# List-scheduled attention and MoE kernel: the planner is told of shared banks of the score tiles, and two due times are moved

## Chip, core, metric

One NeuronCore of one Trainium2 chip runs the whole program. The metric is device time in microseconds (us), median of the runs; less is better.

## What is computed

Two batches, 8 heads, 768 positions, 64 features per head. Queries and keys are each assigned to one of 16 clusters of their head, attention is allowed only inside a cluster, and the result goes through two MLP blocks without a residual:

```python
mask = q_assign[:, :, :, None] == k_assign[:, :, None, :]
scores = np.where(mask, scale * np.matmul(q, k.transpose(0, 1, 3, 2)), -1e9)
attn = softmax(scores); x = attn @ v            # (2, 8, 768, 64) -> (1536, 512)
h = x @ w_in                                     # 512 -> 2048
x = piecewise_quadratic(h) @ w_out               # 2048 -> 512
out = ((x @ w1) * (x @ w2) @ w3) @ w_out2        # 512 -> 1024 -> 1024 -> 512
```

The weights arrive as 64-bit floats and are turned into 32-bit ones on the chip. w3 and w_out2 are multiplied together once (into `wp`).

## The kernel before

**Work.** For each batch there are four units (pairs of heads) and, in each unit, 12 score tiles of 128 queries by 768 keys: 48 score tiles a batch. A score tile s goes through a chain. TensorE writes the scores into PSUM, four matmuls (`s`, L819). VectorE takes the row maximum (`smax`, L827), GpSimd turns it into a bias (`sbias`, L832), ScalarE takes the exponent out of PSUM into the SBUF tile P (`sexp`, L840). In the first batch TensorE then transposes P back into the same PSUM tile, six matmuls (`spT`, L857), and ScalarE or VectorE copies that to `pt` (`sT`, L372 or L374), which frees the PSUM tile. Twelve such tiles end in two products with v (`pv`, L923) with their normalisers (`ro`, L906).

Beside it the first batch's stage holds 16 matmul groups of eight for w3 times w_out2 (`wp`, L1152), the conversion of those weights (L1061 to L1094), and, for the second batch's mask, two groups `am` (L526) with a VectorE chain behind each (`ah`, L540 to L570; its step 4 is two matmuls, L562). `am`, `ah` step 4 and the transposes of v (`vpT`, L750) use PSUM tiles of the same ring as the scores. Matmuls on the identity with nothing to do with the result (L474) keep TensorE occupied where it has no other work early on.

After the first batch's attention, its MLP blocks run on TensorE together with the second batch's attention, then the second batch's MLP blocks (L1208).

**PSUM.** The first batch's ring `("sc", 0)` has four tiles of 768 fp32 columns. `banks` (L292) cuts them in pairs out of tiles of three banks of 512 columns: the first of a pair has bank 1 and half of bank 2, the second the other half of bank 2 and bank 3. So the two tiles of a pair share a bank. The second batch's ring has two tiles with banks of their own. The semaphores, which the framework adds when the program is built, keep apart two engines on one bank of such a tile, whichever halves they use.

**Order.** Every step is entered with `add(...)`: a name, the engines that may do it with a cost in us, a due time, its needs, and what it takes from and frees in rings of buffers. `Plan.order` plays the program through with these costs. Whenever an engine is free it starts the ready step with the earliest due time; a step that isn't ready (`can`) is passed over. What comes out is a fixed order of instructions for each engine's queue, and a queue runs strictly in that order on the chip. The plan knows needs and rings. It does not know of shared banks.

**Due times.** Score tile s of the first batch is due at `slot(s)`, in equal steps from T_A0 = 14 to T_H[0] - 10 = 150 (2.83 each); its later steps are due 1 to 3.5 later. Scores of the second batch are due from T_H[0] - 6 = 154 to T_X1 = 390. `wp` products are due from 45 on, every 7.5. The second batch's mask steps are due from T_A1 = 115 on (keys) and 118 (queries), their eight loads on the SP queue (`al`, L518) 4 earlier; each load waits until the splits of the first batch's unit that sits in the same buffer are done. MLP steps of the first block are due in 56 equal steps from T_H[0] = 160 to T_H[1] = 435, those of the second from 435 to 660.

Of the kernel before, what the change touches and what calls it, by code (L numbers as in the profile page):

```python
# [36 lines left out]
class Plan:  # L37
# [17 lines left out]
    def __init__(self, rings):  # L55
        self.rings, self.ops, self.names, self.last = dict(rings, lane=self.LANES), [], {}, {}

    def add(self, name, engines, due, fn, needs=(), takes=(), frees=(), behind=None, moves=()):

        assert name not in self.names, name
        engines = {e: c if isinstance(c, tuple) else (c, 0.0) for e, c in engines.items()}
        self.names[name] = len(self.ops)
        lanes = [("lane", (name, i)) for i in range(len(moves))]
        prev = self.last.get(behind) if behind else None
        if behind:
            self.last[behind] = len(self.ops)
        lags = {}
        for x in needs:  # L70
            lag, x = x if isinstance(x[0], float) else (0.0, x)
            lags[x] = max(lag, lags.get(x, 0.0))
        self.ops.append([name, engines, due, fn, lags, list(takes) + lanes, list(frees) + lanes, prev, moves])

    def order(self):
        ops, n = self.ops, len(self.ops)
# [9 lines left out]
        engines = ("DMA", "PE", "ACT", "DVE", "POOL")  # L86
# [9 lines left out]
        ring_free = data_free = port_free = self.FIRST  # L96
        done, out, started, now = [], [], [False] * n, self.FIRST

        def can(i):
            if ready_at[i] > now or (ops[i][7] is not None and not started[ops[i][7]]):  # L100
                return False
            need = {}
            for r, _ in ops[i][5]:
                need[r] = need.get(r, 0) + 1
            for r, m in need.items():
                t, size = taken[r], self.rings[r]
                if len(t) + m > size:
                    for x in t[max(0, len(t) - size):max(0, len(t) - size + m)]:
                        if freed.get((r, x), 1e9) > now:
                            return False  # L110
            return True

        def soon(e, i):

# [9 lines left out]
        while len(out) < n:  # L124
            again = True
            while again:
                again = False
                for e in queue:
                    if free_at[e] > now:
                        continue  # L130
                    skipped, pick = [], None
                    while queue[e]:
                        it = heapq.heappop(queue[e])
                        if started[it[1]]:
                            continue
                        if can(it[1]) and not (ops[it[1]][8] and issue_free[e] > now):
                            pick = it
                            break
                        skipped.append(it)
                    for it in skipped:  # L140
                        heapq.heappush(queue[e], it)
                    if pick is None:
                        continue
                    if now < self.START and soon(e, pick[1]):
                        heapq.heappush(queue[e], pick)
                        continue
                    i, again = pick[1], True
                    started[i] = True
                    free_at[e] = now + ops[i][1][e][0]
                    if e == "POOL" or (e == "DVE" and ops[i][0][0] in self.PORT):  # L150
                        free_at[e] += max(0.0, port_free - now)
                        port_free = free_at[e]
                    end = free_at[e] + self.LAT.get(e, 0.0)
                    for ring, data in ops[i][8]:
                        ring_free = max(now, ring_free) + ring
                        data_free = max(ring_free + 0.65, data_free) + data
                        end = max(end, data_free + 0.95)
                    if ops[i][8]:
                        issue_free[e] = ring_free
                    for r, x in ops[i][5]:  # L160
                        taken[r].append(x)
                    heapq.heappush(done, (end, i, 0))
                    out.append((now, len(out), i, e))
            if not done:
                assert all(started), "the rings are too small"
                break
            now = min([done[0][0]] + [t for t in (*free_at.values(), *issue_free.values()) if t > now])
            while done and done[0][0] <= now:
                t, i, who = heapq.heappop(done)
                if not who:  # L170
                    for x in ops[i][6]:
                        holds[x] -= 1
                        if not holds[x]:
                            freed[x] = t
                for k, lag in [(who, 0.0)] if who else users[i]:
                    if lag:
                        heapq.heappush(done, (t + lag, i, k))
                        continue
                    waits[k] -= 1
                    if not waits[k]:  # L180
                        ready_at[k] = t
                        for e, (_, late) in ops[k][1].items():
                            heapq.heappush(queue[e], (ops[k][2] + late, k))
# [5 lines left out]
def cluster_attention_moe_kernel(  # L189
# [121 lines left out]
    plan = Plan(RINGS)  # L311
# [5 lines left out]
        "xs": ROW, "xr": ROW, "os": ROW,  # L317
    }

    def add(name, engines, due, fn, needs=(), takes=(), frees=(), behind=None, moves=None):  # L320
        kind = name if isinstance(name, str) else name[0]
        if moves is None:
            moves = MOVES.get(kind, ()) if "DMA" in engines else ()
        plan.add(name, engines, due, fn, needs, takes, frees, behind, moves)

    T = {}

# [63 lines left out]
    N_IDLE, N_IDLE1 = 90, 30  # L391
    W_SIDE = 1
    LAG_W, LAG_RO, LAG_RI, LAG_K2 = 0.5, 0.5, 1.5, 0.5
    T_AA, T_A1 = 14.0, 115.0
    T_A0, T_W, DT_W = 14.0, 45.0, 7.5
    T_H = [160.0, 435.0, 660.0]
    T_X1 = 390.0


# [192 lines left out]
    for b in range(B):  # L592
        u0 = b * NP
        s0 = T_A1 if b else slot(0) - T_AA
        for wi, w in enumerate("kq"):
            t = s0 + 3.0 * wi
            for j in range(NP):
# [2 lines left out]
                    ("al", b, w, j), {"DMA": 0.5}, t + 0.3 * j - 4.0, raw_load(b, w, j, "a"),  # L600
                    [(x, j, h) for x in left for h in range(2)] + [("qh0", j)] if b else [],
                )
            add(("am", b, w), {"PE": 2.7}, t + 0.9, a_mm(b, w, range(NP)), ["c_put"] + [("al", b, w, x) for x in range(NP)], [(("sc", 0), ("a", b, w))])
            steps = [("DVE", 0.95), ("DVE", 0.87), ("DVE", 0.87), ("DVE", 0.87), ("PE", 0.66 if b == 0 else 0.45), ("DVE", 0.87)]
            if w == "q":
                steps.append(("ACT", 0.83))
            for st, (e, c) in enumerate(steps):
                needs = [("ah", b, w, st - 1)] if st else [("am", b, w)]
                if st == 1 and w == "q":
                    needs.append(("ah", b, "k", 2))  # L610
                add(
                    ("ah", b, w, st), {e: c}, t + 1.5 + 0.1 * st, a_hot(b, w, st), needs,
                    {0: [(("P", 0), ("a", b, w))], 2: [(("phl", 0), ("a", b, w))], 4: [(("sc", 0), ("a2", b, w))],
                     5: [(("P", 0), ("m", w))] if b else []}.get(st, []),
                    {0: [(("sc", 0), ("a", b, w))], 2: [(("P", 0), ("a", b, w))],
                     5: [(("phl", 0), ("a", b, w)), (("sc", 0), ("a2", b, w))]}.get(st, []),
                )
            if b:
                add(("ap", w), {"DMA": 0.5}, t + 2.5, a_put(w), [("ah", b, w, 5 + "kq".index(w))], frees=[(("P", 0), ("m", w))])
# [142 lines left out]
    for u, (b, j) in enumerate(units):  # L762
# [28 lines left out]
        p = slot(u * NG * NS + NS - 1)  # L791
        add(("vl", u), {"DMA": 0.5}, p - 14.0, v_load(u), ([("s", u * NG * NS - V_AHEAD)] if u else [("al", 0, "q", NP - 1)]), [("raw", ("v", u))])
        if whole(u):
            add(("vpT", u), {"PE": 0.65}, p - 3.0, v_pT(u), [("vl", u), "c_put"], [(("sc", b), ("v", u))], [("raw", ("v", u))])
            add(
                ("vT", u), {"ACT": 0.73, "DVE": (0.87, LATE)}, p - 2.0, v_put(u), [("vpT", u)], [("vn", u)],
                [(("sc", b), ("v", u))],
            )
            continue
        add(("vm", u), {"DVE": 1.4}, p - 8.0, v_max(u), [("vl", u)])  # L800
# [48 lines left out]
    def by_pe(s):  # L849
        return s % PE_EVERY[s // NU] == 0  # L850
# [128 lines left out]
    for u, (b, j) in enumerate(units):  # L979
        for g in range(NG):  # L980
            for r in range(NS):
# [5 lines left out]
                    [("k2", u, h), ("klo", u, h)] + ([("k2h", u, h), ("q1h", u, h)] + ([("qh0", u)] if h else []) if by_copy(u) else []),  # L987
                    [(("sc", b), s)],
                    [((x, b), (u, h)) for x in ("k1", "q1", "kq2")] if t == NQ - 1 and g == NG - 1 else [],
                )  # L990
                add(("smax", s), {"DVE": 0.87}, p + 1.0, s_max(s, b), [("s", s)])
                add(("sbias", s), {"POOL": 0.3}, p + 1.0, s_bias(s), [("smax", s)])
                add(
                    ("sexp", s), {"ACT": 0.89}, p + 2.0, s_exp(s, u, g, h, t), [("sbias", s)],
                    [(("P", b), s)] if by_pe(s) else [],
                )
                key, first = ("pt", (u, g, h)), [("pt", (u, g, h))] if t == 0 else []
                hi, lo = {"ACT": 0.73, "DVE": (0.87, LATE)}, {"DVE": 0.88}
                if by_pe(s):
                    add(("spT", s), {"PE": 0.65}, p + 3.0, s_pT(s, b), [("sexp", s), "c_put"], frees=[(("P", b), s)])  # L1000
                    if whole(u):
                        add(("sT", s), hi, p + 3.5, s_hi(s, u, g, h, t), [("spT", s)], first, [(("sc", b), s)], behind=key)
                        continue
                    add(("shi", s), hi, p + 3.5, s_hi(s, u, g, h, t), [("spT", s)], first, behind=key)
                    add(("sT", s), lo, p + 4.2, s_lo(s, u, g, h, t), [("shi", s)], frees=[(("sc", b), s)])
# [413 lines left out]
```

## Time and profile before

| | |
|---|---|
| median of 3 runs | 792.83 us (791.03 to 793.93) |
| profiled execution | 791.59 us |
| its span, first to last instruction | 789.6 us, so 1.99 us lie around it |
| TensorE busy in the span | 758.0 us (96%) |
| VectorE, ScalarE, GpSimd busy | 568.6 (72%), 448.8 (57%), 216.5 us (27%) |
| mean granted TensorE clock | 0.996 of full speed |

In the profile PE is TensorE's matmuls, DVE VectorE, ACT ScalarE, POOL GpSimd, SPq the SP queue. L819 is line 819 of the kernel. Idle time is given with the instruction whose end released it. A queue's idle time matters where its engine sets the end, here TensorE nearly throughout.

### The profile page before, as it was taken

Reading aid. Unit: us, or ns where it says so; the run is one execution under the profiler, and the core shown is the slowest. Engines: PE = TensorE matmul, PEld = TensorE weight load, DVE = VectorE, ACT = ScalarE, POOL = GpSimd, SP = SyncE. Lnnn points to the kernel's source line nnn. Section 1 sums busy time; section 2 is a strip of 40 time slices with the busy share of each in tenths; the row PEclk is TensorE's granted clock in tenths of the full one; section 3 lists DMA queues with packets and bytes.
Section 4 is the critical chain, followed back from the end, with each engine's and each line's share of the span. In section 5 each row is a group of like instructions: output and inputs, shape, how many; then the busy total and the mean of one; then the engine's idle time right before and its main releaser. Section 6 shows DMA issues by size and latency. Waiting matters only on the chain.

```text
span 789.6 us, 12412 instructions
## 1 busy us (share of the span) xinstructions
PE 758.0 (96%) x4593; PEld 665.0 (84%) x4593; DVE 568.6 (72%) x935; ACT 448.8 (57%) x804; POOL 216.5 (27%) x251
## 2 busy tenths in 40 slices
PE   7989899989999999999999999999999999999998
PEld 5864555545669898999989898999999999999998
DVE  7889686778789788999899999842655564644520
ACT  7478687754677566687677766631544353323311
POOL 0223233421243334555445544210211021000000
PEclk9999999999999999999999999999999999999999
DMA  8416564646378458777776888663222212221211
GB/s 335 143 47 217 176 202 139 226 129 203 121 211 165 94 127 156 206 199 160 209 215 178 224 200 203 167 182 108 72 68 55 73 60 68 68 66 54 67 61 61
DMA packets 100973, 112.78 MB, mean 143 GB/s; under 512 B 61489, under 2 KB 69681, under 8 KB 100913
## 3 DMA queue, kind: packets, MB, share of 16 engines
q1 hardware_dynamic: 78768, 52.48, 26.4%
q10 hardware_dynamic: 22144, 59.52, 24.9%
q8 instruction: 36, 0.59, 0.3%
q14 instruction: 25, 0.20, 0.1%
HBM read 73.70 MB, written 20.19 MB: 119 GB/s over the span
## 4 chain that ended last, share of the span: by engine, by line
PE 77%; DVE 9%; ACT 5%; issue 3%; DMA 3%; POOL 2%; SPq 0%; ACTq 0%; POOLq 0%; DVEq 0%
PE mo L1208 36%; PE sc L1208 15%; PE sc L819 7%; PE sc L857 4%; PE av L1208 4%; PE mo L1152 3%; PE av L931 3%; PE av L923 3%; DVE nm L827 2%; ACT P L840 2%; ACT pt L372 1%; PE mo L906 1%; DMA pt<-phl 1%; DVE wf L1077 1%; DMA kq<-in_qT_dram 1%
## 5 line engine op out<-in xcount | busy, mean ns | idle before, releaser
L1208 PE MATMUL mo<-X,whl 128*128 128x384 f32 x1188 | 216.3, 337 | 0.4 <-DVE G L377 0.4
L1208 PEld LDWEIGHTS mo<-X,whl 128*128 128x128 f32 x1188 | 205.2, 188 | 2.6 <-DVE G L377 1.0
L377 POOL TENSOR_TENSOR whl<-wf,whl 128x512 fp32r<-128x512 f32 x60 | 79.0, 1318 | 176.4 <-DVE whl L374 44.8
L1208 PE MATMUL mo<-G,whl 128*128 128x384 f32 x660 | 120.2, 337 | 0.0
L1208 PEld LDWEIGHTS mo<-G,whl 128*128 128x128 f32 x660 | 114.0, 188 | 1.6 <-issue 0.6
L827 DVE TENSOR_REDUCE nm<-sc 128x1 f32<-128x768 f32 x96 | 90.9, 951 | 29.8 <-PE sc L819 12.6
L1208 PE MATMUL sc<-X,whl 128*128 128x384 f32 x432 | 76.5, 335 | 0.0
L372 ACT ACTIVATE whl<-wf 128x512 fp32r<-128x512 f32 x69 | 43.5, 632 | 55.7 <-PE mo L1208 30.3
L1208 PEld LDWEIGHTS sc<-X,whl 128*128 128x128 f32 x432 | 75.1, 188 | 0.0
L840 ACT ACTIVATE P<-sc,nm 128x768 f32<-128x768 f32 x64 | 57.5, 900 | 21.1 <-POOL nm L832 11.5
L857 PEld LDWEIGHTS sc<-ident,P 128*128 128x128 f32 x384 | 43.5, 141 | 26.6 <-ACT P L840 10.6
L857 PE MATMUL sc<-ident,P 128*128 128x128 f32 x384 | 52.9, 277 | 12.8 <-ACT P L840 5.8
L832 POOL TENSOR_SCALAR nm<-nm 128x1 f32<-128x1 f32 x96 | 29.1, 303 | 131.4 <-DVE nm L827 123.5
L372 ACT ACTIVATE pt<-sc 128x768 f32<-128x768 f32 (+1 forms) x55 | 44.1, 811 | 35.0 <-PE sc L857 19.1
L819 PE MATMUL sc<-k,q 128*128 128x512 f32 (+1 forms) x192 | 55.6, 371 | 6.3 <-ACT pt L372 2.6
L1152 PE MATMUL mo<-wo,wf 128*128 128x512 f32 x128 | 58.3, 599 | 0.7 <-ACT rb L372 0.7
L1094 POOL TENSOR_TENSOR wf<-wf,w 128x512 int32<-128x512 int32 x32 | 44.2, 1382 | 53.7 <-DVE wf L1077 33.9
L377 DVE TENSOR_TENSOR whl<-wf,whl 128x512 fp32r<-128x512 f32 x52 | 36.9, 709 | 23.6 <-ACT whl L372 22.1
L819 PE MATMUL sc<-kq 80*128 80x512 f32 (+1 forms) x192 | 49.7, 340 | 0.0
L374 DVE CAST whl<-wf 128x512 fp32r<-128x512 f32 x43 | 18.8, 438 | 42.0 <-PE mo L1208 23.1
L1077 DVE SCALAR_TENSOR_TENSOR wf<-w,wf 128x512 uint32<-128x512 uint32 x64 | 48.1, 753 | 0.3
L819 PEld LDWEIGHTS sc<-k,q 128*128 128x128 f32 x192 | 31.6, 190 | 16.7 <-ACT pt L372 4.4
(155 smaller groups left out, 1220.0 us busy)
## 6 DMA issues: line engine op xcount, KB each, us to landing
wf<-wd ACTq DMA_DIRECT2D x64, 256.0 KB, 2.6
w<-in_w_out_dram ACTq DMA_DIRECT2D x24, 512.0 KB, 3.9
wd<-wf SPq DMA_DIRECT2D x48, 256.0 KB, 3.4
w<-in_w3T_dram ACTq DMA_DIRECT2D x16, 512.0 KB, 4.0
w<-in_w_in_dram ACTq DMA_DIRECT2D x16, 512.0 KB, 4.2
w<-in_w_dram ACTq DMA_DIRECT2D x16, 512.0 KB, 4.2
wf<-wp ACTq DMA_DIRECT2D x16, 256.0 KB, 2.9
kq<-in_kT_dram SPq DMA_DIRECT2D x8, 384.0 KB, 4.6
```

What stands on the lines that cost most here:

```text
L372: nc.scalar.activation(out=out, in_=in_, func=AF.Copy)
L377: (nc.gpsimd if e == "POOL" else nc.vector).tensor_tensor(out=out, in0=a, in1=b, op=ALU.subtract)
L819: nc.tensor.matmul(ps[:, n], q[0:n_rows, q0:q0 + 128], k[0:n_rows, n], start=first, stop=not first)
L827: nc.vector.tensor_reduce(out=nm, in_=T[("sc", b), s], axis=AX.X, op=ALU.max, negate=True)
L832: nc.gpsimd.tensor_scalar(out=tl[s, "nm"], in0=tl[s, "nm"], scalar1=SCALE, scalar2=EC, op0=ALU.mult, op1=ALU.add)
L840: nc.scalar.activation(out=new(("P", b), s).rearrange("p n s -> p (n s)") if by_pe(s) else T[("sc", b), s], in_=T[("sc", b), s], func=AF.E ...
L857: nc.tensor.transpose(T[("sc", b), s][:, c], p[:, c], ident)
L923: nc.tensor.matmul(acc[rows(h), :], vn[:, kt, rows(h)], T["pt", (u, g, h)][:, :, kt, :], start=(kt == 0), stop=(kt == KT - 1),)
L1077: nc.vector.scalar_tensor_tensor(out=w, in0=T[w64, i][:, :, 1], scalar=0xC0000000, in1=w, op0=ALU.bitwise_and, op1=ALU.bitwise_or)
L1094: nc.gpsimd.tensor_tensor(out=w, in0=w, in1=T[w64, i].bitcast(I32)[:, :, 0], op=ALU.add)
L1152: nc.tensor.matmul(acc, w[:, k4 * 128:(k4 + 1) * 128], wo2[:, hf * 4 + k4], start=(hf == 0 and k4 == 0), stop=(hf == 1 and k4 == 3),)
L1208: nc.tensor.matmul(acc, w[:, a, k4 * 128:(k4 + 1) * 128], rhs(c, k4), start=(first and k4 == 0 and n == 0), stop=(last and k4 == 3 and n = ...
```

## The change

No step is added or taken away. A step may name a tile in its new argument `near`. While the plan is made, a TensorE step with `near` isn't started as long as a step of another engine with `near` on the same pair of tiles is running, and the other way round. Two readers are not kept apart. It holds for the first batch's ring only. Steps with `near`: `am`, `ah` steps 0, 4 and 5, `vpT`, `vT`, `s`, `smax`, `sexp`, `spT`, `sT`. Besides, T_A1 goes from 115 to 105 and T_H[0] from 160 to 155 (and with it the first batch's scores to 14 to 145, 2.73 each, the second's to 149 to 390).

```diff
-    def add(self, name, engines, due, fn, needs=(), takes=(), frees=(), behind=None, moves=()):
+    def add(self, name, engines, due, fn, needs=(), takes=(), frees=(), behind=None, moves=(), near=None):
...
-        def can(i):
+        def can(i, e):
...
                         if freed.get((r, x), 1e9) > now:
                             return False
+            if ops[i][9]:
+                r, x = ops[i][9]
+                if until.get((r, pair(r, x), e != "PE"), 0.0) > now:
+                    return False
             return True
+
+        until = {}
+
+        def pair(r, x):
+            return (taken[r].index(x) if x in taken[r] else len(taken[r])) % self.rings[r] // 2
...
                     for r, x in ops[i][5]:
                         taken[r].append(x)
+                    if ops[i][9]:
+                        r, x = ops[i][9]
+                        until[r, pair(r, x), e == "PE"] = end
...
-        plan.add(name, engines, due, fn, needs, takes, frees, behind, moves)
+        plan.add(name, engines, due, fn, needs, takes, frees, behind, moves, (near if near and near[0] == ("sc", 0) else None))
...
-    T_AA, T_A1 = 14.0, 115.0
+    T_AA, T_A1 = 14.0, 105.0
     T_A0, T_W, DT_W = 14.0, 45.0, 7.5
-    T_H = [160.0, 435.0, 660.0]
+    T_H = [155.0, 435.0, 660.0]
...
+                    near=(("sc", 0), ("a" if st == 0 else "a2", b, w)) if st in (0, 4, 5) else None,
...
+                    near=(("sc", b), s),
                 )
-                add(("smax", s), {"DVE": 0.87}, p + 1.0, s_max(s, b), [("s", s)])
+                add(("smax", s), {"DVE": 0.87}, p + 1.0, s_max(s, b), [("s", s)], near=(("sc", b), s))
```

`am`, `vpT`, `vT`, `sexp`, `spT` and the first batch's `sT` get the same `near=` argument.

## Rows read from the trace of the kernel before

**Rows 1.** Busy time by stretch: us, busy of PE, PEld, DVE, ACT, POOL; clock, DMA share, GB/s
```profile
31.00:232.00 201.00, 181.64 (x996) 112.30 (x995) 158.28 (x246) 138.58 (x236) 66.00 (x84) 0.99 0.52 166
232.00:500.00 268.00, 264.70 (x1732) 246.82 (x1731) 246.60 (x394) 188.40 (x347) 119.08 (x132) 1.00 0.75 180
```

**Rows 2.** Waits of PE, 31 to 232 us: total us, times, longest us
```profile
PE sc L857 <- ACT P L840: 5.2, 8, 1.1
PE sc L819 <- ACT pt L372: 2.6, 4, 0.9
PE sc L857 <- DVE P L540: 2.6, 1, 2.6
PE sc L857 <- DVE nm L827: 2.3, 2, 1.5
PE sc L857 <- ACT pt L372: 2.1, 3, 1.7
PE sc L819 <- DVE nm L827: 1.5, 3, 0.5
PE sc L819 <- ACT P L840: 0.9, 1, 0.9
PE sc L819 <- DVE pt L374: 0.7, 2, 0.4
```

**Rows 3.** Timeline: start us, us, engine, line, operation [idle before <- releaser]
```profile
111.72 0.89 ACT L840 ACTIVATE P<-sc,nm 128x768 f32<-128x768 f32 x1
112.75 0.61 PE L819 MATMUL sc<-k,q 128*128 128x512 f32 x2 [0.92 <-ACT P L840]
```

**Rows 4.** Timeline of PE: the first and the last of three waits for an own result
```profile
45.33 0.88 PE L857 MATMUL sc<-ident,P 128*128 128x128 f32 x6 [0.72 <-ACT P L840]
...
67.03 1.76 PE L857 MATMUL sc<-ident,P 128*128 128x128 f32 x12 [1.14 <-ACT P L840]
```

**Rows 5.** Timeline of the longest wait, 164 to 176 us
```profile
164.42 0.59 ACT L372 ACTIVATE wf<-mo 128x512 f32<-128x512 f32 x1
...
167.57 0.98 DVE L540 STREAM_TRANSPOSE P<-sc 128x768 f32<-128x768 f32 x1 [0.17 <-ACT P L840]
...
168.61 1.27 PE L857 MATMUL sc<-ident,P 128*128 128x128 f32 x6 [2.61 <-DVE P L540]
...
170.97 4.29 PE L1152 MATMUL mo<-wo,wf 128*128 128x512 f32 x8
```

**Rows 6.** Busy time by stretch, as in rows 1, right behind that wait
```profile
170.00:172.00 2.00, 2.00 (x6) 1.29 (x6) 0.80 (x1) 0.73 (x1) 0.00 (x0) 0.50 0.76 250
```

**Rows 7.** Timeline of PE: the same three steps as in rows 5 at another place
```profile
127.42 0.88 PE L857 MATMUL sc<-ident,P 128*128 128x128 f32 x6
...
128.83 3.60 PE L1152 MATMUL mo<-wo,wf 128*128 128x512 f32 x8
```

**Rows 8.** Timeline of PE: the first and last of ten waits with a product ready
```profile
55.50 0.87 PE L857 MATMUL sc<-ident,P 128*128 128x128 f32 x6 [0.75 <-ACT P L840]
...
219.22 1.53 PE L857 MATMUL sc<-ident,P 128*128 128x128 f32 x12 [0.90 <-ACT P L840]
```

**Rows 9.** Waits of ACT and of DVE, 31 to 232 us: total us, times, longest us
```profile
ACT pt L372 <- DVE nm L827: 14.0, 6, 5.8
...
DVE nm L827 <- ACT P L840: 7.8, 7, 2.5
```

**Rows 10.** Timeline of the SP queue: the last load for the second batch's mask
```profile
154.07 0.33 SPq L518 DMA_DIRECT2D kq<-in_qT_dram  x1
```

**Rows 11.** Timeline, 213 to 223 us: the end of the first batch's attention
```profile
213.37 0.52 PE L819 MATMUL sc<-k,q 128*128 128x256 f32 x2
...
214.08 3.60 PE L1152 MATMUL mo<-wo,wf 128*128 128x512 f32 x8
...
220.59 3.60 PE L1152 MATMUL mo<-wo,wf 128*128 128x512 f32 x8
...
221.50 0.81 ACT L372 ACTIVATE pt<-sc 128x768 f32<-128x768 f32 x1
```

More of the change, by code (lines that the diff above doesn't have):

```diff
@@ L72, in add @@
             lags[x] = max(lag, lags.get(x, 0.0))
-        self.ops.append([name, engines, due, fn, lags, list(takes) + lanes, list(frees) + lanes, prev, moves])
+        self.ops.append([name, engines, due, fn, lags, list(takes) + lanes, list(frees) + lanes, prev, moves, near])
     def order(self):
@@ L135, in order @@
                             continue
-                        if can(it[1]) and not (ops[it[1]][8] and issue_free[e] > now):
+                        if can(it[1], e) and not (ops[it[1]][8] and issue_free[e] > now):
                             pick = it
@@ L318, in cluster_attention_moe_kernel, with add @@
     }
-    def add(name, engines, due, fn, needs=(), takes=(), frees=(), behind=None, moves=None):
+    def add(name, engines, due, fn, needs=(), takes=(), frees=(), behind=None, moves=None, near=None):
         kind = name if isinstance(name, str) else name[0]
@@ L602, in cluster_attention_moe_kernel @@
                 )
-            add(("am", b, w), {"PE": 2.7}, t + 0.9, a_mm(b, w, range(NP)), ["c_put"] + [("al", b, w, x) for x in range(NP)], [(("sc", 0), ("a", b, w))])
+            add(("am", b, w), {"PE": 2.7}, t + 0.9, a_mm(b, w, range(NP)), ["c_put"] + [("al", b, w, x) for x in range(NP)], [(("sc", 0), ("a", b, w))], near=(("sc", 0), ("a", b, w)))
             steps = [("DVE", 0.95), ("DVE", 0.87), ("DVE", 0.87), ("DVE", 0.87), ("PE", 0.66 if b == 0 else 0.45), ("DVE", 0.87)]
@@ L793, in cluster_attention_moe_kernel @@
         if whole(u):
-            add(("vpT", u), {"PE": 0.65}, p - 3.0, v_pT(u), [("vl", u), "c_put"], [(("sc", b), ("v", u))], [("raw", ("v", u))])
+            add(("vpT", u), {"PE": 0.65}, p - 3.0, v_pT(u), [("vl", u), "c_put"], [(("sc", b), ("v", u))], [("raw", ("v", u))], near=(("sc", b), ("v", u)))
             add(
                 ("vT", u), {"ACT": 0.73, "DVE": (0.87, LATE)}, p - 2.0, v_put(u), [("vpT", u)], [("vn", u)],
-                [(("sc", b), ("v", u))],
+                [(("sc", b), ("v", u))], near=(("sc", b), ("v", u)),
             )
@@ L994, in cluster_attention_moe_kernel @@
                     ("sexp", s), {"ACT": 0.89}, p + 2.0, s_exp(s, u, g, h, t), [("sbias", s)],
-                    [(("P", b), s)] if by_pe(s) else [],
+                    [(("P", b), s)] if by_pe(s) else [], near=(("sc", b), s),
                 )
@@ L999, in cluster_attention_moe_kernel @@
                 if by_pe(s):
-                    add(("spT", s), {"PE": 0.65}, p + 3.0, s_pT(s, b), [("sexp", s), "c_put"], frees=[(("P", b), s)])
+                    add(("spT", s), {"PE": 0.65}, p + 3.0, s_pT(s, b), [("sexp", s), "c_put"], frees=[(("P", b), s)], near=(("sc", b), s))
                     if whole(u):
-                        add(("sT", s), hi, p + 3.5, s_hi(s, u, g, h, t), [("spT", s)], first, [(("sc", b), s)], behind=key)
+                        add(("sT", s), hi, p + 3.5, s_hi(s, u, g, h, t), [("spT", s)], first, [(("sc", b), s)], behind=key, near=(("sc", b), s))
                         continue
```

## The prediction

> **What bounds the kernel now.** I began with the busy times by stretch. From 31 to 232 us, the first batch's attention with its `wp` products, TensorE is busy for 181.64 of 201 us; from 232 to 500 us for 264.70 of 268 [rows 1]. So TensorE sets the pace, and what it loses it loses in the first of these stretches: 201 - 181.64 = 19.4 us. The change acts in just that stretch, since only the first batch's ring is named in `near`. VectorE (158.28) and ScalarE (138.58) have more room there, on average.
>
> The second view is the list of TensorE's waits in the stretch [rows 2]. Nearly all of the 19.4 us stand before L819 (scores) and L857 (transposes): 5.2 + 2.6 + 2.6 + 2.3 + 2.1 + 1.5 + 0.9 + 0.7 = 17.9 us. The reader is to see what ended them. A score tile's own chain gives L857 one thing to wait for, its exponent (ACT P L840), and gives L819 one, the copy that frees its tile (L372 or L374). A transpose that waits for a row maximum (DVE nm), for another tile's copy (ACT pt) or for the mask's VectorE transpose (DVE P L540), and scores that wait for a maximum or an exponent, wait for somebody else's read. Those rows are 2.6 + 2.3 + 2.1 + 1.5 + 0.9 = 9.4 us. The timeline shows one: an exponent runs from 111.72 to 112.61, and scores that have no need of it start at 112.75 after 0.92 us of waiting [rows 3]. The other reader sits in the tile that shares the bank. The rest, 5.2 + 2.6 + 0.7 = 8.5 us, can be either. Counting the instructions of each line off against the written order, I find three waits for an own result among them, the first of 0.72 us and the last of 1.14 us [rows 4], 2.4 us in all. So **about 17.9 - 2.4 = 15.5 us are waits on a shared bank**, which the plan did not foresee: it put a step at the head of TensorE's queue that could not start, and what was ready behind it stood still.
>
> **The change, part by part.** No instruction is added or removed, DMAs included; the cost of the planning is paid when the program is built. What changes is order, and here and there which of two engines does a copy.
>
> *The knowledge of pairs.* Where a reader is under way in the pair, the planner passes over the score or transpose and takes another TensorE step. It saves the wait if such a step is ready. I take the `wp` products as the cover, since they write no shared bank. In ten of the waits the next product had its weights ready and its accumulator free by the written order: the first is the 0.75 us before the transpose at 55.50, the last the 0.90 us at 219.22 [rows 8], and the 0.92 us of [rows 3] is one. The largest is the 2.61 us before the transpose at 168.61, ended by L540; the copy that frees the accumulator for the product run at 170.97 was over at 164.42 + 0.59 = 165.01 [rows 5], before the wait began. Together the ten are 7.7 us. For the other 15.5 - 7.7 = 7.8 us I see no product to put there, so I leave them.
>
> *The clock.* Behind that 2.61 us the granted clock was 0.50, the lower of its two levels (1.2 against 2.4 GHz), from 170 to 172 us [rows 6]. Transpose, scores and product took 170.97 + 4.29 - 168.61 = 6.65 us there; the same three took 128.83 + 3.60 - 127.42 = 5.01 us elsewhere [rows 7]. If the wait goes, 1.6 us go with it.
>
> *What it costs.* A product of 3.60 us put first makes a ready score or transpose late, and all that hangs on it: the copy, the freed tile, the next scores. The trace has no price for a tile that is late on purpose. At the least it is nothing, as TensorE works meanwhile; at the most it is the whole 7.7 us, as another wait later. The nearest rows are the waits for own results, which are what lateness costs now: 2.4 us over 48 tiles, 0.05 each [rows 4]. For the ten displaced tiles I take three times that, 0.15 us each: 1.5 us.
>
> *The new waits in the plan.* A reader is now held back too, in the plan, while TensorE writes the pair. The chip does that anyway, so it adds no wait; it moves conversions of weights ahead on VectorE and ScalarE. I count nothing: both have over 40 us free in the stretch [rows 1]. Without that room it would be up to one read, about 0.9 us [rows 3], each time.
>
> *T_A1, 10 earlier.* Eight loads on SP, two `am` groups on TensorE and the mask's chain on VectorE get an earlier due time. The last of the loads went out at 154.07 [rows 10], and each has to wait for the splits of the unit whose buffer it fills; those splits move by 4 at most (slots of 2.73 for 2.83). So most of the 10 cannot be used. Behind a load that waits on the SP queue stand the stores of converted weights, which free the buffers of the next conversion; a load takes 0.33 us there, and eight are 2.6 us of a queue that is nearly empty. Nothing, between -1 and +1 us.
>
> *T_H, 5 earlier.* The second batch's scores and the first MLP block are due 5 earlier together, and their order against each other stays nearly what it was: they start more than 70 us after their due times anyway (154, against the 228 at which this stage is over). Covered by the full TensorE from 232 us on. Nothing, within 1 us either way by a new order.
>
> **The sum.** 7.7 + 1.6 - 1.5 = 7.8 us less. As TensorE works through 264.70 of the next 268 us [rows 1], I carry all of it to the end. The profiled execution took 791.59 us: 783.8. The median shown lies 1.24 us above it, so 785.0 us, 1% less. The most that the mechanism can bring is all 15.5 us and the clock's 1.6, 17.1 in all: 775.7. The least is nothing.
>
> **A rule that speaks against it.** VectorE waits for ScalarE's exponents, 7.8 us in seven waits, and ScalarE's copies for row maxima, 14.0 us in six [rows 9]. These are reads that wait for reads, and the change leaves them out of the plan. The Trainium skill, PSUM — Partial Sum Buffer, on bank collisions, counts two engines' reads of one bank as a collision too, so that reads have to be kept apart as well as a write from a read. The trace agrees with that rule: the two rows are such waits. By it, a plan that keeps only writes from reads is still wrong on the chip; what that would cost is the first rival.
>
> **The rivals.** *Reads against reads (no change).* The plan is true for TensorE but not for its feeders. Their waits, 14.0 and 7.8 us [rows 9], stay, so exponents and copies come later than planned, and the waits on banks turn into waits for own results. Then only the one long wait goes surely, 2.61 + 1.6 = 4.2 us, and half of that is paid back in late tiles: 792.83 - 2.1 = 790.7 us. For it: these waits are as large as TensorE's own. Against: they fall on engines that have 43 and 62 us free, and five of the eight rows of TensorE's waits cannot be waits for an own result at all.
>
> *Given back later (no change).* From 232 to 500 us VectorE is busy for 246.60 of 268 us, 92% [rows 1]. If TensorE comes there 8 us earlier with fewer weights converted ahead, VectorE sets the pace and takes the 7.8 us back: 792.8. Against: its work up to the stage's end shifts with TensorE's, since both go by the same tiles.
>
> *An empty end of the stage (slower).* The products are a stock of 16, and what is used early is missing later. The last scores start at 213.37, the last copy ends at 221.50 + 0.81 = 222.31: a chain of 8.9 us, filled by the two products at 214.08 and 220.59, 7.2 us [rows 11]. If both were moved ahead of the last scores, TensorE would stand for 7.2 us where nothing else is allowed to start, and the lower clock would follow: 7.2 + 1.6. With half of the ten waits saved (3.9), that is 792.83 + 8.8 - 3.9 = 797.7 us. It decides from the point at which no product is left when the 46th tile is written. Against: products are due up to 157.5, later than the last score (145), so the list tends to keep the last ones.
>
> **The numbers.** 0.64 for the forecast, with a range of its own from 778 to 789; 0.16 for reads against reads, 0.09 for given back later, 0.11 for the empty end. A measurement of this kernel tells about 0.5% from no change, 4.0 us. The forecast is faster, the next two are no change (0.25), the last is slower. For 8 in 10 I go from 778, some 2 us above the best that the waits allow, to 796, which takes in both cases of no change and the upper bound of the unknown costs; the rest of the empty end, and a gain near the maximum, are left out.
>
> **What would show it.** Right: TensorE's idle time from 31 us to the end of the first batch's attention falls from 19 to about 11 us; the rows of L857 and L819 released by DVE nm, ACT pt and DVE P shrink most; products stand directly behind the places of the old waits; no stretch after 31 us has a clock of 0.5; the attention of the first batch ends some 8 us earlier, and all that follows is shifted by as much. Reads against reads: the idle time stays near 19 us, with ACT P before L857 as the largest row. Given back: the stage ends 8 us earlier, and TensorE shows new waits for VectorE between 232 and 500 us. Empty end: no L1152 after the last L819 of the stage, and a wait of several us before the last transposes. The forecast is wrong if the stage doesn't get shorter.

## The result, and the profile after

The changed kernel takes **785.66 us** (median of 4 runs, 784.62 to 786.52) against 792.74 (4 runs, 791.03 to 793.93): 0.9912 of the time before, 95% interval 0.9890 to 0.9934. Its profiled execution took 784.62 us with a span of 782.9; before it was 791.59 and 789.6. The spans differ by 6.7 us, and that difference is what the views below share out. In the changed kernel all lines are 14 to 16 higher: L834 is `s`, L872 `spT`, L842 `smax`, L855 `sexp`, L386 and L388 the copies, L554 the mask's VectorE transpose, L1168 `wp`, L1224 the MLP.

To compare the same work I cut the span at two starts that every kernel has: the first scores, and the first product with w_out (the first matmul `mo<-G`). Between them stand the same 306 transposes, 128 `wp` matmuls and 144 MLP matmuls in both kernels. First the row of that start, before and after:

```profile
269.44 1.84 PE L1208 MATMUL mo<-G,whl 128*128 128x384 f32 x9
```

```profile
265.16 2.01 PE L1224 MATMUL mo<-G,whl 128*128 128x384 f32 x10
```

The busy times between the two starts, before (columns as in [rows 1]):

```profile
30.89:269.44 238.55, 218.54 (x1245) 146.69 (x1244) 192.31 (x300) 165.82 (x287) 78.38 (x101) 0.99 0.55 162
```

and after:

```profile
32.17:265.16 232.99, 217.33 (x1247) 145.81 (x1246) 196.49 (x307) 163.04 (x284) 76.09 (x99) 1.00 0.54 165
```

The stretch is 5.56 us shorter. TensorE's idle time in it falls from 238.55 - 218.54 = 20.0 to 232.99 - 217.33 = 15.7 us, so 4.3 us are waits. The other 1.2 us are busy time; most of it goes with the clock (0.99 to 1.00), and 0.4 us are less time in matmuls on the identity (7.8 to 7.4 us). But it begins 32.17 - 30.89 = 1.3 us later, and behind it, from the first w_out product to the end, 520.2 us (789.6 - 269.4) became 517.7 (782.9 - 265.2). **The 6.7 us are 5.6 - 1.3 + 2.4**, and the last term was not in the prediction.

TensorE's waits after, from 31 to 226 us, to hold against [rows 2] (total us, times, longest):

```profile
PE sc L872 <- ACT P L855: 6.1, 8, 1.3
PE sc L834 <- DVE nm L842: 2.4, 2, 2.0
PE sc L834 <- ACT P L855: 1.2, 2, 0.7
PE sc L872 <- DVE nm L842: 1.2, 1, 1.2
PE sc L834 <- ACT pt L386: 1.1, 2, 0.6
PE sc L872 <- DVE P L554: 0.9, 2, 0.7
...
PE sc L834 <- DVE pt L388: 0.6, 1, 0.6
```

The rows that can only be somebody else's read fall from 9.4 us to 2.4 + 1.2 + 1.2 + 0.9 = 5.7. Transposes no longer wait for another tile's copy (2.1 us before), and the wait for L554 fell from 2.6 to 0.9. The row for exponents grew from 5.2 to 6.1. The seven rows together are 13.5 us, where [rows 2] had 17.9. VectorE's and ScalarE's waits for each other's reads shrank as well ([rows 9] had 14.0 and 7.8), though the plan does not know of them:

```profile
ACT pt L386 <- DVE nm L842: 5.1, 2, 4.2
...
DVE nm L842 <- ACT P L855: 2.1, 4, 1.0
```

The clock, where it had been 0.50 [rows 6], is full in the stretches around the mask's steps; the first column pair is the stretch and its length, and the third figure from the right the clock:

```profile
165.00:170.00 5.00, 4.83 (x19) 2.67 (x20) 4.93 (x8) 1.59 (x3) 0.00 (x0) 1.00 0.00 0
170.00:175.00 5.00, 3.91 (x23) 2.09 (x23) 4.96 (x12) 3.88 (x6) 1.68 (x3) 1.00 0.54 184
```

The late start shows in VectorE's timeline. Before, the transpose of the first mask group ran as soon as the matmuls of both groups were over:

```profile
13.83 0.98 DVE L540 STREAM_TRANSPOSE P<-sc 128x768 f32<-128x768 f32 x1 [0.32 <-PE sc L526]
```

After, it stands behind one more step of VectorE, a split of q that itself waits for ScalarE, both transposes run together behind that, and the mask and the first scores come later:

```profile
15.16 0.95 DVE L391 TENSOR_TENSOR q<-kq,kq 64x768 fp32r<-64x768 f32 x1 [1.70 <-ACT kq L386]
16.14 1.85 DVE L554 STREAM_TRANSPOSE P<-sc 128x768 f32<-128x768 f32 x2
```

The plan gives each `am` group 2.7 us. In the profiled executions both together take 4.70 us in the changed kernel and 3.73 before. The plan lets no read into the pair until it believes the second group done, and starts another step on VectorE instead.

### The profile page after: what moved, and what is told of

Its sections match the earlier page's. It is cut to its first block, busy times and chain, and to the rows that moved or that the text cites. A ratio compares the mean times of both kernels' runs of the same rounds, so it can differ in the third digit from the quotient of the medians.

```text
span 782.9 us, 12419 instructions
## 1 busy us (share of the span) xinstructions
PE 758.3 (97%) x4592; PEld 664.5 (85%) x4593; DVE 570.6 (73%) x938; ACT 444.7 (57%) x800; POOL 218.0 (28%) x252
## 4 chain that ended last, share of the span: by engine, by line
PE 78%; ACT 7%; DVE 7%; issue 4%; DMA 2%; POOL 1%; ACTq 1%; SPq 1%; DVEq 0%; POOLq 0%
PE mo L1224 38%; PE sc L1224 15%; PE sc L834 6%; PE av L938 4%; PE sc L872 4%; PE av L1224 4%; PE mo L1168 3%; PE av L946 3%; DVE nm L842 2%; ACT P L855 2%; ACT pt L386 1%; PE mo L921 1%; DMA raw<-in_vT_dram 1%; ACT kq L386 1%; ACT wf L1077 1%
## 5 line engine op out<-in xcount | busy, mean ns | idle before, releaser
L1224 PE MATMUL mo<-X,whl 128*128 128x384 f32 x1188 | 216.9, 337 | 0.4 <-DVE G L391 0.4
L1224 PEld LDWEIGHTS mo<-X,whl 128*128 128x128 f32 x1188 | 205.1, 188 | 3.2 <-DVE G L391 0.9
L391 POOL TENSOR_TENSOR whl<-wf,whl 128x512 fp32r<-128x512 f32 x62 | 81.3, 1312 | 191.9 <-DVE whl L388 52.6
L1224 PE MATMUL mo<-G,whl 128*128 128x384 f32 x660 | 120.0, 337 | 0.0
L1224 PEld LDWEIGHTS mo<-G,whl 128*128 128x128 f32 x660 | 114.0, 188 | 1.8 <-DVE phl L391 0.3
L842 DVE TENSOR_REDUCE nm<-sc 128x1 f32<-128x768 f32 x96 | 90.0, 948 | 10.2 <-PE sc L834 3.1
L1224 PE MATMUL sc<-X,whl 128*128 128x384 f32 x432 | 76.5, 335 | 0.0
L1224 PEld LDWEIGHTS sc<-X,whl 128*128 128x128 f32 x432 | 75.1, 188 | 0.0
L386 ACT ACTIVATE whl<-wf 128x512 fp32r<-128x512 f32 x66 | 41.7, 631 | 55.4 <-PE mo L1224 26.5
L855 ACT ACTIVATE P<-sc,nm 128x768 f32<-128x768 f32 x64 | 57.4, 900 | 22.2 <-POOL nm L847 13.3
L872 PEld LDWEIGHTS sc<-ident,P 128*128 128x128 f32 x384 | 43.0, 141 | 24.3 <-ACT P L855 13.2
L834 PE MATMUL sc<-k,q 128*128 128x512 f32 (+1 forms) x192 | 55.0, 367 | 6.4 <-DVE nm L842 2.4
L872 PE MATMUL sc<-ident,P 128*128 128x128 f32 x384 | 52.2, 276 | 8.7 <-ACT P L855 6.5
L386 ACT ACTIVATE pt<-sc 128x768 f32<-128x768 f32 (+1 forms) x54 | 43.3, 810 | 27.7 <-PE sc L872 16.3
L1168 PE MATMUL mo<-wo,wf 128*128 128x512 f32 x128 | 57.7, 593 | 0.2 <-POOL wf L1110 0.2
L388 DVE CAST whl<-wf 128x512 fp32r<-128x512 f32 x46 | 19.5, 424 | 44.4 <-PE mo L1224 25.6
L391 DVE TENSOR_TENSOR whl<-wf,whl 128x512 fp32r<-128x512 f32 x50 | 34.5, 690 | 23.2 <-ACT whl L386 21.9
L1093 DVE SCALAR_TENSOR_TENSOR wf<-w,wf 128x512 uint32<-128x512 uint32 x64 | 49.9, 783 | 0.3
L834 PE MATMUL sc<-kq 80*128 80x512 f32 (+1 forms) x192 | 49.4, 338 | 0.0
L1077 ACT ACTIVATE wf<-w 128x512 f32<-128x512 f32 x64 | 42.4, 673 | 6.2 <-issue 2.0
```

The lines of the kernel that those rows point to most:

```text
L386: nc.scalar.activation(out=out, in_=in_, func=AF.Copy)
L391: (nc.gpsimd if e == "POOL" else nc.vector).tensor_tensor(out=out, in0=a, in1=b, op=ALU.subtract)
L834: nc.tensor.matmul(ps[:, n], q[0:n_rows, q0:q0 + 128], k[0:n_rows, n], start=first, stop=not first)
L842: nc.vector.tensor_reduce(out=nm, in_=T[("sc", b), s], axis=AX.X, op=ALU.max, negate=True)
L855: nc.scalar.activation(out=new(("P", b), s).rearrange("p n s -> p (n s)") if by_pe(s) else T[("sc", b), s], in_=T[("sc", b), s], func=AF.E ...
L872: nc.tensor.transpose(T[("sc", b), s][:, c], p[:, c], ident)
```

## The experiments

My theory: TensorE's waits on shared banks were cut, and that is the gain. The rivals: the moved due times made it, or the one order that came out; reads against reads still hold something back. Times are medians, of 4 runs for the kernels before and changed and of 5 or more for the others; ratios are to the kernel before on the same chip. The last three columns are of each kernel's one profiled execution: TensorE's idle time between the first scores and the first w_out product (the length of that stretch less TensorE's busy time in it), the start of the first w_out product, and from there to the end of the span.

| kernel | time, us | ratio (95%) | TensorE idle, first part | first w_out product at | rest |
|---|---|---|---|---|---|
| before | 792.7 | | 20.0 | 269.4 | 520.2 |
| changed | 785.7 | 0.9912 (0.9890 to 0.9934) | 15.7 | 265.2 | 517.7 |
| 1 pairs alone | 788.8 | 0.9948 (0.9936 to 0.9960) | 14.3 | 264.8 | 522.2 |
| 2 due times alone | 798.1 | 1.0061 (1.0044 to 1.0077) | 18.2 | 271.3 | 525.0 |
| 3 reads kept apart too | 793.3 | 1.0007 (0.9994 to 1.0020) | 13.7 | 266.0 | 526.5 |
| 4 three tiles, own banks | 783.3 | 0.9885 (0.9870 to 0.9901) | 9.8 | 259.3 | 521.6 |
| 5 pairs, T_A1 put back | 790.3 | 0.9976 (0.9954 to 0.9997) | 14.1 | 264.2 | 523.7 |
| 6 pairs, T_H[0] put back | 789.3 | 0.9957 (0.9942 to 0.9972) | 15.5 | 267.5 | 520.4 |
| 7 only mask reads known | 798.1 | 1.0075 (1.0054 to 1.0096) | 22.2 | 276.7 | 519.9 |
| 8 three tiles, due times moved | 793.7 | 1.0013 (0.9998 to 1.0029) | 13.0 | 268.6 | 524.9 |
| 9 before, T_X1 = 395 | 806.9 | 1.0177 (1.0140 to 1.0214) | 19.3 | 269.7 | 533.2 |
| 10 changed, T_X1 = 395 | 798.4 | 1.0073 (1.0046 to 1.0100) | 15.3 | 266.3 | 532.7 |
| 11 changed, first mask free | 794.1 | 1.0015 (0.9993 to 1.0038) | 15.3 | 266.8 | 523.7 |
| 12 three tiles, T_X1 = 395 | 789.7 | 0.9973 (0.9943 to 1.0002) | 10.6 | 259.5 | 526.6 |

**1. Pairs alone.**

```diff
-    T_AA, T_A1 = 14.0, 105.0
+    T_AA, T_A1 = 14.0, 115.0
-    T_H = [155.0, 435.0, 660.0]
+    T_H = [160.0, 435.0, 660.0]
```

> The changed kernel with both due times put back (T_A1 = 115, T_H[0] = 160), so that the planner's knowledge of pairs stands alone. If that knowledge made the gain (my theory), the time is within 2 us of the changed kernel: 784 to 788 us. If the moved due times made it, or the one lucky order that they lead to with it, it is 790 to 795 us, although TensorE's waits on shared banks between 31 us and the stage's end are as few as in the changed kernel.

788.8 us, just outside the first range and short of the second. It reaches the first w_out product at 264.8, as early as the changed kernel, and loses behind it. TensorE's waits from 232 to 506 us:

```profile
PE mo L1224 <- DVE G L391: 4.4, 5, 1.6
PE sc L834 <- DVE phl L391: 1.5, 1, 1.5
PE sc L834 <- DVE pt L391: 1.4, 1, 1.4
PE av L946 <- DMA pt<-phl: 0.5, 1, 0.5
```

7.8 us, against 1.9 in the changed kernel. So the knowledge of pairs alone makes the gain of the first part, and another order makes or unmakes some us of the second.

**2. Due times alone** (in the kernel before).

```diff
-    T_AA, T_A1 = 14.0, 115.0
+    T_AA, T_A1 = 14.0, 105.0
-    T_H = [160.0, 435.0, 660.0]
+    T_H = [155.0, 435.0, 660.0]
```

> The kernel before with the two due times moved (T_A1 = 105, T_H[0] = 155) and no knowledge of pairs. My theory: 791 to 794 us, with TensorE's idle time in the first batch's attention still near 19 us. If the due times made the gain: 785 to 788 us.

798.1 us, slower than before and than either forecast. TensorE's idle time in the first part is 18.2 us, near the 19 expected. By themselves the due times are no gain. Behind the first part there is a wait that is neither in the kernel before nor in the changed one:

```profile
PE sc L819 <- DVE phl L377: 3.3, 2, 2.5
PE mo L1208 <- POOL whl L377: 1.2, 1, 1.2
```

and behind its 2.5 us the clock falls for some us:

```profile
404.00:408.00 4.00, 4.00 (x19) 3.98 (x18) 3.94 (x8) 2.44 (x6) 0.91 (x2) 0.74 0.66 125
```

**3. Reads kept apart too** (in the changed kernel; the start of a unit's sums is made independent of which tile comes first).

```diff
-                if until.get((r, pair(r, x), e != "PE"), 0.0) > now:
+                if any(until.get((r, pair(r, x), o), 0.0) > now for o in ("PE", "ACT", "DVE") if o != e):
...
-                        until[r, pair(r, x), e == "PE"] = end
+                        until[r, pair(r, x), e] = end
```

> The changed kernel, and the planner also keeps a VectorE read and a ScalarE read of one pair apart. If reads against reads take back part of the gain (the first rival of the prediction), this brings another 3 to 5 us: 781 to 783 us, and VectorE's waits for ACT P and ScalarE's waits for DVE nm shrink. If they fall on engines with room, the time stays within 2 us of 785.7.

The waits in question are all but gone: from 31 to 226 us ScalarE's copies no longer wait for row maxima (5.1 us in the changed kernel), and VectorE's maxima wait 0.4 us for exponents (2.1). Still the first w_out product starts at 266.0, not earlier than in the changed kernel. The busy times between the two starts, as in [rows 1]:

```profile
32.50:266.01 233.51, 219.79 (x1271) 150.15 (x1270) 204.94 (x320) 153.11 (x272) 73.69 (x97) 0.99 0.55 167
```

TensorE's idle time is 13.7 us, 1.9 less than in the changed kernel, and its busy time 2.5 more, at a clock of 0.99. So by this execution these reads hold back about 2 us of TensorE's time at most, and another order may be the reason for those. The total of 793.3, outside both ranges, is lost behind that point (526.5), with the same rows as in experiment 2, 3.3 and 1.2 us.

**4. Three tiles with banks of their own** (in the kernel before).

```diff
-    BANKS = {("sc", 0): 4, "av": 1, ("mo", 0): 1, ("sc", 1): 2, ("mo", 1): 3, ("mo", 2): 8}
+    BANKS = {("sc", 0): 3, "av": 1, ("mo", 0): 1, ("sc", 1): 2, ("mo", 1): 3, ("mo", 2): 8}
-    PER = (2, 1)
+    PER = (1, 1)
```

> The kernel before with three score tiles in the first batch's ring, each in two banks of its own, instead of four that share banks in pairs. No wait on a shared bank is left, and one tile less is in flight. If the shared banks cost the 15 us that I read from the waits, and three tiles suffice, this is some 8 us faster than before, 783 to 787 us. If the number of tiles is the bound, waits for an own result take their place (L819 for a copy, L857 for its exponent) and it is 793 to 800 us.

783.3 us. The first w_out product starts at 259.3, 10.1 us earlier than before and 5.9 earlier than with the pairs. All waits of TensorE on score tiles from 31 to 222 us:

```profile
PE sc L819 <- ACT pt L372: 4.1, 6, 1.5
PE sc L857 <- ACT P L840: 3.6, 6, 1.0
```

Only the two waits that a tile's own chain can give are left, 7.7 us for 17.9 in [rows 2]. The busy times between the two starts:

```profile
30.84:259.29 228.45, 218.70 (x1278) 152.46 (x1276) 198.38 (x305) 161.41 (x284) 74.12 (x98) 0.99 0.56 169
```

TensorE's idle time falls by 10.2 us, from 20.0 to 9.8. With these due times, then, the shared banks cost 10 us net of one tile less in flight, and the planner's knowledge gets back about four to five of them. Experiment 8 shows that the 10 us hold for these due times only.

**5 and 6. One due time put back** (in the changed kernel: T_A1 = 115; then T_H[0] = 160 instead).

> The changed kernel with T_A1 alone put back to 115 (T_H[0] stays 155). The changed kernel and the one with the pairs alone differ by 3 us, which lies in TensorE's waits for VectorE between 232 and 506 us (1.9 against 7.8 us). If the moved T_H[0] keeps VectorE ahead there, this is 784 to 787 us with under 3 us of such waits. If T_A1 or the chance of one order does it, it is 787 to 791 us.

> The changed kernel with T_H[0] alone put back to 160 (T_A1 stays 105). If T_H[0] is what helps the later stretch: 787 to 791 us, with 6 to 8 us of TensorE's waits for VectorE between 232 and 506 us. If T_A1 is: 784 to 787 us. If both this and the run with T_A1 put back are as slow as the pairs alone, neither due time does it by itself and the order's chance is left.

790.3 and 789.3 us. Neither due time by itself gives the 517.7 us of the rest; the case named last in the second text has come. In experiment 5 the rest has the rows of experiment 2 again (3.3 and 1.2 us), in experiment 6 this one in their place:

```profile
PE sc L834 <- DVE phl L391: 2.0, 1, 2.0
```

**7. Only the mask's reads known** (pairs alone, `near` kept for four kinds of steps).

```diff
-(near if near and near[0] == ("sc", 0) else None))
+(near if near and near[0] == ("sc", 0) and kind in ("am", "ah", "s", "spT") else None))
```

> The kernel with the pairs alone (both due times as before), but only the mask's steps, the scores and the transposes carry the pair; maxima, exponents and copies do not. If the one long wait for the mask's VectorE transpose and the lower clock behind it (4.2 us) are most of the gain, this is 788 to 790 us. If the many short waits on maxima, exponents and copies matter too, it stays at 790 to 793 us, with TensorE's idle time in the stage above 16 us.

798.1 us, worse than either. The first w_out product alone comes 7.3 us later than before: 1.8 us are a later start of the first scores, 2.2 more idle time and 3.4 more busy time at a lower clock (0.97, where the kernel before has 0.99):

```profile
32.65:276.74 244.09, 221.89 (x1233) 147.68 (x1231) 192.48 (x305) 165.48 (x286) 76.22 (x99) 0.97 0.54 158
```

TensorE's waits from 31 to 238 us, the longest:

```profile
PE sc L872 <- ACT pt L386: 4.5, 5, 2.0
PE sc L872 <- ACT P L855: 3.9, 6, 1.2
PE sc L834 <- ACT pt L386: 2.8, 3, 0.9
PE sc L872 <- DVE nm L842: 2.3, 3, 1.2
PE sc L872 <- DVE P L554: 1.9, 1, 1.9
```

The waits on maxima and copies are all there, and the mask's own is 1.9 us still. So this kernel did not remove the long wait that it was to single out, and it can't tell how much of the gain that wait is. It shows that knowledge of these steps alone is no gain.

**8. Three tiles and the moved due times.**

> Three tiles with banks of their own, no knowledge of pairs, and the two moved due times (T_A1 = 105, T_H[0] = 155). If the due times help whatever the tiles, by easing the stretch from 232 to 506 us, this gains 2 to 3 us on the three tiles alone: 780 to 782 us. If they helped only by one order: 782 to 790 us.

793.7 us: the due times cost the three tiles 10 us. The rest is 524.9 us, again with the rows of experiment 2, and the first w_out product comes 9.3 us later too. The busy times between the two starts:

```profile
31.05:268.57 237.52, 224.53 (x1283) 155.17 (x1281) 201.00 (x318) 157.24 (x273) 71.98 (x97) 0.97 0.52 162
```

Against experiment 4 that is 3.2 us more idle time and 5.8 more busy time, at a clock of 0.97 for 0.99. So the due times are no help in themselves, and the worth of banks of one's own depends on them: against experiment 2, with the same due times and shared banks, TensorE's idle time falls by 5.2 us (18.2 to 13.0), and the first w_out product comes only 2.7 us earlier (271.3 to 268.6). The changed kernel, with these due times and shared banks that the planner knows of, reaches it at 265.2 and is faster than three tiles here.

**9 and 10. T_X1 = 395**, in the kernel before and in the changed one. TensorE's order is the same up to the eleventh MLP product.

```diff
-    T_X1 = 390.0
+    T_X1 = 395.0
```

> The kernel before with the second batch's last due time moved by 5 (T_X1 = 395): the order up to the end of the first batch's attention stays, only the order behind it changes. No theory has a reason for a gain or a loss. If the chance of one order behind 232 us is worth some us, the part up to the 200th matmul of the MLP keeps its 281 us and the rest moves by 1 to 5 us either way; if that part of the kernel is settled by TensorE's work, the total stays within 1 us of 792.8.

> The same move of T_X1 in the changed kernel. The stretch up to the 200th matmul of the MLP keeps what the pairs gained (276.6 us). If the 2.5 us that the changed kernel gains behind it come from one order, they are lost here and the time is 787 to 790 us; if they come from the pairs, it stays at 784 to 787 us.

806.9 and 798.4 us. The first parts stay (269.7 and 266.3); the rest grows from 520.2 to 533.2 and from 517.7 to 532.7, far more than I had allowed. The waits behind 232 us in the kernel before with T_X1 = 395:

```profile
PE av L931 <- DMA pt<-phl: 5.4, 1, 5.4
PE sc L819 <- DVE pt L377: 3.2, 1, 3.2
PE mo L1208 <- DVE X L377: 2.1, 2, 1.1
```

The clock fell again, here by the wait of 5.4 us, which ended at 458.96:

```profile
459.00:463.00 4.00, 4.00 (x32) 2.33 (x34) 0.19 (x1) 1.73 (x4) 0.00 (x0) 0.60 0.91 236
```

In the changed kernel it is other waits for VectorE (4.0 before MLP products, 2.6 before scores). The 2.4 us that the changed kernel had won there are lost, and 12.5 more.

**11. The first batch's mask free** (in the changed kernel, `am` and `ah` carry `near` only for the second batch).

> The changed kernel, but the first batch's own mask steps do not carry the pair. In all kernels with the pairs the first scores start 1.2 to 1.6 us later than before (32.2 against 30.9 us), since the plan holds the mask's first VectorE transpose back until it believes both of the mask's matmul groups done. If that is the reason, the first scores start at 30.9 us again. The total would then be 784 to 785 us by that alone; another order behind it may move it by 3 us either way.

The mask's transpose runs at 14.07, ahead of that split of q again, and the first scores start at 30.96: the cause of the late start is confirmed. (A lower clock can do the same: in experiment 9, without the pairs, the two `am` groups took 5.17 us at a clock near 0.5, and the first scores started at 32.01.) The earlier start was worth nothing by the end of the first part, though. The first w_out product comes at 266.8, 1.7 us later than in the changed kernel, the rest is 523.7 and the time 794.1: the order behind it came out worse.

**12. Three tiles, T_X1 = 395.**

> Three tiles with banks of their own and T_X1 = 395. The stretch up to the 200th matmul of the MLP stays at 271 us, 10 us less than before and 6 less than in the changed kernel. The rest is an order that I can't foresee: 779 us if it comes out as in the changed kernel, 783 as with three tiles, up to 788.

789.7 us: the first part stays (259.5), the rest is 526.6, beyond the range that I gave.

The fastest kernel is the three tiles of experiment 4. Its advantage over the changed kernel in the first part is 5.9 us. In the total it is 2.4 us, and the two ratios' intervals overlap a little, so that the totals do not clearly tell them apart.

## Why the prediction was right, and where it was not

785.0 us were forecast and 785.66 measured. The sign and the mechanism hold. That the sum fits so closely is luck: waits forecast 1.9 us too large and a late start of 1.3 us that was not foreseen are made up by 2.4 us from the rest, which no term foresaw. Without those 2.4 us it would be some 788 us.

**The mechanism holds.** There are three comparisons with equal due times: before against 1, 2 against changed, 9 against 10. With the pairs known, the kernel is 4.5, some 12 and 8.5 us faster, and the first w_out product comes 4.6, 6.1 and 3.4 us earlier. That second figure is the part that can be put down to the pairs, as the parts behind it differ by order. An order can move the first part too, by 9.3 us between experiments 4 and 8, so the steadier sign is TensorE's idle time there: 18.2 to 20.0 us in the three kernels with shared banks that the plan doesn't know of (before, 2 and 9), 13.7 to 15.7 in the seven with the pairs known (the changed kernel and experiments 1, 3, 5, 6, 10 and 11), 9.8 to 13.0 in the three without shared banks (4, 8 and 12). These groups do not overlap. Experiment 7, whose plan knows the pairs for some steps only, has 22.2. Experiment 4 shows from the other side that the shared banks were what TensorE lost time on.

**The waits: 7.7 - 1.5 = 6.2 us forecast, 4.3 measured.** This term of the sum was too large. The predicted idle time of about 11 us in the stage came out at 15.7, in a somewhat longer stretch that had 20.0 before. What failed is mainly the payback: 0.15 us for each displaced tile, taken from waits for own results. The trace tells own results and neighbours apart by the order in which transposes and exponents follow each other. In experiment 4, where no bank is shared, that count gives own results alone, as it should. This is a wait for an own exponent in the changed kernel, the 21st tile's transpose behind the 21st tile's exponent:

```profile
107.80 0.90 ACT L855 ACTIVATE P<-sc,nm 128x768 f32<-128x768 f32 x1 [0.85 <-DVE nm L842]
...
108.85 0.87 PE L872 MATMUL sc<-ident,P 128*128 128x128 f32 x6 [0.94 <-ACT P L855]
```

Of the eight waits for exponents (6.1 us) six are for the own exponent, 4.4 us, where before there were two, 1.9 us. With one wait for a tile's own copy each (0.6 us) own results cost 5.0 us now, for 2.4 before: a payback of 2.6 us for 1.5. What is left of the 13.5 us, 8.5, are waits on a shared bank, for 15.5 before: 7.0 us saved for 7.7. They were not all cut: a wait of 1.96 us for a neighbour's row maximum is new. Why the plan still runs into these is not shown.

**The clock: 1.6 us forecast, 1.2 of busy time measured.** Right, as near as one execution tells; no stretch between the two starts had the lower clock. That it stayed full behind the new wait of 1.96 us was luck, as the last section shows.

**"I count nothing" for readers held back** was wrong. The first scores came 1.3 us later for it, as experiment 11 shows. What that costs by the end is not shown, since the order of experiment 11 differs behind it as well. That the plan's cost of `am` is too high (2.7 us each, 4.70 measured for both) may add to it; that was not tested apart. I had looked for VectorE's room in the stage, but before the first scores VectorE's mask chain is itself the path.

**"Nothing, within 1 us" for the moved due times** was wrong in size. With the pairs known, the due times bring some 3 us (experiment 1 against the changed kernel); without them they lose 5 us (experiment 2). Five other kernels with T_H[0] = 155 and T_X1 = 390 have a rest of 523.7 to 526.5 us (experiments 2, 3, 5, 8, 11); the changed kernel has 517.7 and stands alone. That is where the 2.4 us come from. The full TensorE that I named as cover is no cover: VectorE and the transposing transfers of the second batch's tiles release it late in some orders. That this order is a good one is shown; why just this combination leads to it isn't.

**The rivals.** Reads against reads: it did not come, as TensorE's idle time fell to 15.7 us and did not stay near 19. The waits of reads for reads existed, and experiment 3 leaves about 2 us at most for them. Given back later: it did not happen in the changed kernel. In experiments 1, 3, 5 and 11, with the pairs known, the rest is 2.0 to 6.3 us longer than before, with new waits for VectorE. But experiments 2 and 8, without that knowledge, have the same rows of 3.3 and 1.2 us as experiments 3, 5 and 11, though TensorE comes there later than in those. So these waits need no TensorE that comes early, and the order is the likelier cause. An empty end: it shows a little. The last `wp` product starts at 209.07, and behind it TensorE fills with matmuls on the identity (L488) and waits for 1.26 us; it isn't the 7.2 us of that rival.

```profile
209.07 3.60 PE L1168 MATMUL mo<-wo,wf 128*128 128x512 f32 x8
213.05 0.87 PE L872 MATMUL sc<-ident,P 128*128 128x128 f32 x6 [0.38 <-ACT P L855]
213.76 2.40 PE L488 MATMUL av<-ident 128*128 128x128 f32 x20
217.41 1.53 PE L872 MATMUL sc<-ident,P 128*128 128x128 f32 x12 [1.26 <-ACT P L855]
```

## What to carry to other kernels

Read who released a wait and ask whether the waiting step needs that result at all; where it does not, look for something that the two share, here a bank. Fewer buffers with banks of their own can then be worth more (10 us of the first part here) than a schedule that steps around the sharing (4 to 5). Try both, as the order decides too: with the other due times the three tiles were the slower of the two (793.7 against 785.7 us). In a kernel whose order comes out of a list schedule, cut the span at a step that all versions have, and judge a change by the part it can reach: a due time moved by 5 us shifted the rest of this kernel by 13. A total that agrees with the forecast does not prove the terms of the sum.

## What the runs showed that I had not expected

The same wait can cost the clock or not. In the changed kernel and in experiment 6 TensorE stands for 1.96 us at the same place. The wait and the next scores, in the changed kernel:

```profile
62.38 0.62 PE L834 MATMUL sc<-k,q 128*128 128x256 f32 x2 [1.96 <-DVE nm L842]
...
66.97 0.61 PE L834 MATMUL sc<-k,q 128*128 128x512 f32 x2 [0.53 <-ACT pt L386]
```

and in experiment 6:

```profile
62.58 0.62 PE L834 MATMUL sc<-k,q 128*128 128x256 f32 x2 [1.96 <-DVE nm L842]
...
67.87 0.62 PE L834 MATMUL sc<-k,q 128*128 128x512 f32 x2 [0.70 <-ACT pt L386]
```

Right behind it the granted clock stays full in the changed kernel:

```profile
64.00:66.00 2.00, 1.18 (x11) 0.94 (x10) 1.79 (x3) 1.79 (x4) 1.83 (x3) 1.00 0.96 388
```

and is at its lower level in experiment 6, where 18 transposes in a row take 3.67 us:

```profile
64.00:66.00 2.00, 2.00 (x11) 1.93 (x10) 1.63 (x3) 1.50 (x3) 1.83 (x3) 0.50 0.85 344
```

Elsewhere in the changed kernel 18 in a row take 2.13 us. At this place in the changed kernel the last six of the 18 wait 0.82 us for their exponent, so that part of the slower clock is hidden: from the scores behind the wait to the next scores it is 66.97 - 62.38 = 4.59 us at the full clock and 67.87 - 62.58 = 5.29 at the lower one. Experiment 1 is like the changed kernel here (1.96 us of wait, full clock, 4.59), experiment 10 like experiment 6 (2.11 us, lower clock, 5.33). A wait of that length is therefore a risk, worth about 0.7 us here, and not a fixed price.
